# A decode attention kernel with streamed caches: the products with V eight slots later, Wq as one transfer in K's ring, Wo in fewer and larger pieces

## The chip, the core and the metric

The kernel runs on one core of a Trainium2 chip. The metric is the device time of one execution in microseconds. Three runs of the kernel before gave 201.97, 202.30 and 202.43 us (median 202.3). Times inside the text are microseconds from the start of the span of one profiled execution.

## The reference

A batch of eight tokens `x` (8 x 1 x 512) goes through a layer norm, then through two units, and the result is `x + s * g`:

```
xn = layernorm(x)
q  = xn @ wq                               # 32 heads of 128, four to each of 8 K/V heads
s  = softmax(q k^T * 128**-0.5) v @ wo     # over the last 2048 of 8192 cached positions
g  = silu((sigmoid(xn @ w_gate) * (xn @ w_up)) @ w_down)     # width 1792
out = x + s * g
```

All inputs are bf16. The windows of the two caches are 32 MB each (8 batches x 8 heads x 2048 positions x 128), Wq and Wo 4 MB each, and the three matrices of the gate 1.75 MB each: some 81 MB to be read, and little arithmetic on each byte.

## The kernel before, in words

**Tiles and rings.** K comes in eight tiles of 4 MB, K0 to K7, four to each half of the batch (four batches); a partition of a K tile is one run of 32 KB in memory. V comes in sixteen tiles of 2 MB, V0 to V15, two to each batch, with runs of 16 KB. K tiles live in a ring of three buffers of 32 KB a partition (`kring`), V tiles in a ring of four buffers of 16 KB (`vring`). Wq is read in two transfers into two of V's buffers; the gate's weights, Wd (`w_down`) and Wo follow K through K's ring. A buffer is free when the tile that was in it has been `released`, that is, when the last instruction that reads it has been put out.

**The order of loads.** All loads but x's are issued by SyncE (SP) in one queue, in an order that a sorted list fixes (lines 188 to 198): K tile i is due at slot 8i, V tiles four slots apart from the slot `PV_AT` at which their products begin. SP issues in that order and waits at each load for its buffer, so a load that waits holds back all loads behind it, in either ring. The gate's weights stand ahead of the last two V tiles, Wd and Wo at the end. Wo is read in eight pieces of 8, 8, 4, 4, 4, 2, 1 and 1 of its 32 rows a partition (1 KB a row).

**The slots.** The schedule is written by hand: one loop over slots (line 656) puts out a slot's work for every engine, in this order:

- the maximum of a K tile whose scores are complete (`soft_max_part`), and at `EXP_AT` (36 and 68) the exponentials of a batch half (`soft_exp`, ScalarE);
- just ahead of `PV_AT`, the masks (`soft_mask`, line 544, VectorE, eight instructions in two slots), which write the probabilities in the layout that the products need; there is one buffer for them, so the second half's masks wait until the first half's products are done;
- `k_turn`: one of eight in-place transposes of a K tile on VectorE (line 446); at `EXP_AT + 1`, `soft_turn`, the transposes of the probabilities;
- `qk`, four slots behind: four score products of K's tile on TensorE (line 461);
- `pv_sum` of the V tile that was completed in the slot before (TensorE line 621, then VectorE line 630), and `pv`: a quarter of the products of one V tile (line 600); after the fourth quarter ScalarE evicts the sums (line 611);
- at `EXP_AT + 2`, `soft_spread` (line 522, with evictions on ScalarE, line 530); in the slot ahead of `PV_AT`, `soft_den`, the denominators.

A V tile takes four slots, a K tile eight. In before `PV_AT` is 41 and 75: the products of the first batch half, V0 to V7, run in slots 41 to 72 beside the second half's K tiles, those of V8 to V15 from slot 75 on. Each engine works in this order, and SP's loads are put out at the end of each slot.

**Beginning and end.** The q projection (line 387) multiplies each half of Wq when it has landed; `q_out` lays the result out for the scores. After the last V tile `o_rows` lays out the attention output, `unit_out` multiplies by Wd (line 362), and 64 products with Wo (line 707) follow Wo's pieces as they land; two VectorE instructions and the store end the program.

Of the kernel before, what the change touches and what calls it, by code (L numbers as in the profile page):

```python
# [10 lines left out]
def kernel(  # L11
# [13 lines left out]
    nc = tc.nc  # L25
    P = 128
    B, _, D = A_x.shape
    _, Hkv, Sk, Dh = A_k_cache.shape
    Hq = A_wq.shape[1] // Dh
# [3 lines left out]
    KT = D // P  # L33
# [8 lines left out]
    GL = 4  # L42
    NG = Hkv // GL
# [17 lines left out]
    VSET = NT // HB  # L61
    QK_LAG = 4
    EXP_AT = [SET * (hb + 1) + QK_LAG for hb in range(HB)]
    PV_AT = [EXP_AT[0] + 5]
    for hb in range(1, HB):
        PV_AT.append(max(EXP_AT[hb] + 5, PV_AT[hb - 1] + VSET * NJ + 2))

# [36 lines left out]
    def load(dst, src, q=None):  # L104
        if q is None:
            q = nc.sync
        q.dma_start(out=dst, in_=src)  # L107

    def k_tile(shape, name):
        return kring.tile(shape, bf16, name=name, tag="kring", align_bytes=ALIGN)  # L110

    def v_tile(shape, name):
        return vring.tile(shape, bf16, name=name, tag="vring", align_bytes=ALIGN)
# [1 line left out]
    x_bf = work.tile([B, D], bf16, name="x_bf")  # L115
    nc.scalar.dma_start(out=x_bf[:], in_=A_x.flatten_outer_dims())

    wq_view = A_wq.rearrange("(p kt) n -> p kt n", kt=KT)
    KH = KT // 2
    wq_sb = []  # L120
    for kh in range(2):
        t = v_tile([P, KH, Hq * Dh], f"wq_sb{kh}")
        load(t[:], wq_view[:, kh * KH : (kh + 1) * KH, :])
        wq_sb.append(t)

    k_tiles = {}
    v_tiles = {}
# [41 lines left out]
    def load_wo():  # L169
        t = k_tile([P, KW, D], "wo_sb")  # L170
        for t0, t1 in (
            (0, 8),
            (8, 16),
            (16, 20),
            (20, 24),
            (24, 28),
            (28, 30),
            (30, 31),
            (31, 32),
        ):  # L180
            load(t[:, t0:t1, :], wo_view[:, t0:t1, :])
            for k in range(t0, t1):
                wo_parts[k] = t[:, k, :]
# [4 lines left out]
    loads = [  # L188
        (kind, i)
        for _, kind, i in sorted(  # L190
            [(KTS * i, 0, i) for i in range(NKT)]
            + [(NJ * (i % VSET) + PV_AT[i // VSET], 1, i) for i in range(NT)]
        )
    ]
    loads[-2:-2] = [(2, 0)]
    loads = loads + [(2, 1), (2, 2)]
    k_order = [x for x in loads if x[0] != 1]
    v_order = [(4, 0), (4, 1)] + [x for x in loads if x[0] == 1]
    loads_done = [0]
    released = set()  # L200

    def issue_loads():
        while loads_done[0] < len(loads):
            x = loads[loads_done[0]]
            kind, i = x
            order, n = (v_order, VRING) if kind == 1 else (k_order, KRING)
            at = order.index(x)
            if at >= n and order[at - n] not in released:
                break
            if kind == 0:  # L210
                load_k(i)
            elif kind == 1:
                load_v(i)
            else:
                (load_gate_up, load_down, load_wo)[i]()
            loads_done[0] += 1
# [40 lines left out]
    for c in range(NCOL):  # L257
        nc.tensor.matmul(
            x2_ps[32 * c : 32 * (c + 1), :],
            lhsT=ident[:B, :32],  # L260
            rhs=x_bf[:, DC * c : DC * (c + 1)],
            start=True,
            stop=True,
            tile_position=(0, 32 * c),
            skip_group_check=True,
# [3 lines left out]
    xnT_sb = work.tile([P, KT, 32], bf16, name="xnT_sb")  # L269
# [107 lines left out]
    def q_projection():  # L377
        HW = rep * Dh
        q_ps = [
            psum.tile([P, HW], f32, name=f"q_ps{gg}", tag="s_ps") for gg in range(NG)  # L380
        ]
        for kh in range(2):
            for gg in range(NG):
                for kt in range(KH * kh, KH * (kh + 1)):
                    for gl in range(GL):
                        h0 = HW * (GL * gg + gl)
                        nc.tensor.matmul(  # L387
                            q_ps[gg][32 * gl : 32 * (gl + 1), :],
                            lhsT=xnT_sb[:, kt, :],
                            rhs=wq_sb[kh][:, kt % KH, h0 : h0 + HW],  # L390
                            start=(kt == 0),
                            stop=(kt == KT - 1),
                            tile_position=(0, 32 * gl),
                            skip_group_check=True,
                        )
        return q_ps

    def q_out(gg, q_ps, on_dve):
        HW = rep * Dh
        q_sb = ppool.tile([P, HW], bf16, name="q_sb", tag="pp")  # L400
        nc.scalar.copy(  # L401
            out=q_sb[:].rearrange("p (y e w) -> p y e w", e=2, w=32),
            in_=q_ps[:].rearrange("p (y w e) -> p y e w", e=2, w=32),
        )
        qT_sb = ppool.tile([P, HW], bf16, name="qT_sb", tag="pp")
        nc.vector.transpose(out=qT_sb[:], in_=q_sb[:])  # L406
        for gl in range(GL):
            for Q in range(NQ):
                h = GL * gg + gl
                c0 = rep * NQ * (h % 2) + rep * Q  # L410
                out = qz_sb[32 * Q : 32 * (Q + 1), :, h, :, c0 : c0 + rep]
                in_ = qT_sb[32 * gl : 32 * (gl + 1), :].rearrange(
                    "p (r y b) -> p b y r", r=rep, b=32
                )[:, Q:B:NQ]
                if Q in on_dve:
                    nc.vector.tensor_copy(out=out, in_=in_)
                else:
                    nc.scalar.copy(out=out, in_=in_)  # L418

    q_tiles = q_projection()  # L420
    q_out(0, q_tiles[0], (0, 1))
    released |= {(4, 0), (4, 1)}
    issue_loads()

    s_tiles = {}
# [87 lines left out]
    def soft_spread(hb):  # L513

        pt = pt_of.pop(hb)[:].rearrange("p c (y m) -> p c y m", y=2)
        pc = ppool.tile([P, NG, NQ, CH, rep], bf16, name="pc_bf", tag="pp")
        for gg in range(NG):
            for ch in range(2):
                c = slice(CB * ch, CB * (ch + 1))
                pT_ps = psum_a.tile([P, CB, NQ, rep], f32, name="pT_ps", tag="acc_ps")  # L520
                for y in range(2):
                    nc.tensor.matmul(  # L522
                        pT_ps[:],
                        lhsT=spread[:, gg, y].rearrange("p k g -> p (k g)"),
                        rhs=pt[:, c, y, :],
                        start=(y == 0),
                        stop=(y == 1),
                        skip_group_check=True,
                    )
                nc.scalar.copy(  # L530
                    out=pc[:, gg, :, c, :].rearrange("p q c r -> p c q r"),
                    in_=pT_ps[:],
                )
        pc_of[hb] = pc

    def soft_mask(hb, gg):

        if gg == 0:
            pT_of[hb] = work.tile(
                [P, NG, NQ * CB, GL, 2 * rep], bf16, name="pT_sb", tag="pT_sb"  # L540
            )
        pc = pc_of[hb][:, gg].rearrange("p q (c e) r -> p (q c) (e r)", e=2)
        for gl in range(GL):
            nc.vector.tensor_scalar(  # L544
                out=pT_of[hb][:, gg, :, gl, :],
                in0=pc,
                scalar1=Hm[:, gl : gl + 1],
                scalar2=None,
                op0=ALU.mult,
            )  # L550
# [104 lines left out]
    KSLOT = NKT * KTS  # L655
    for t in range(PV_AT[-1] + VSET * NJ):
        u = -1
        for hb, at in enumerate(PV_AT):
            if 0 <= t - at < VSET * NJ:
# [3 lines left out]
        for hb in range(HB):  # L663
            if t == EXP_AT[hb]:
                soft_exp(hb)
            for gg in range(NG):
                if t == PV_AT[hb] - NG + gg:
                    soft_mask(hb, gg)
# [13 lines left out]
        for hb in range(HB):  # L682
            if t == EXP_AT[hb] + 2:
                soft_spread(hb)
            if t == PV_AT[hb] - 1:
                soft_den(hb)
# [18 lines left out]
    for k in range(KW):  # L705
        for c in range(NCOL):
            nc.tensor.matmul(  # L707
                a_ps[32 * c : 32 * (c + 1), :],
                lhsT=o2_sb[:, k, :],
                rhs=wo_parts[k][:, DC * c : DC * (c + 1)],  # L710
                start=(k == 0),
                stop=(k == KW - 1),
                tile_position=(0, 32 * c),
                skip_group_check=True,
# [41 lines left out]
```

## Time and profile before

| | |
|---|---|
| median of three runs | 202.3 us |
| the profiled execution's own time | 201.77 us |
| its span, first to last instruction | 200.0 us |
| mean granted TensorE clock | 0.867 |
| read from memory | 81.01 MB, 405 GB/s over the span |
| products with V begin | 84.1 us |
| first exponentials of the second half | 130.9 us |
| V8's products done (first tile of the second half) | 150.6 us |
| Wd landed, last Wo product | 186.7 us, 196.9 us |

The page shows each engine's busy time, then forty slices of 5 us with the busy tenths of each engine, the granted TensorE clock, the DMA engines' share and rate. A chain follows the last instruction back to what released it. A row of the timeline gives start, length, engine, line, operation and names; the brackets behind it say how long the engine had been idle and what ended that. An issue's time to landing is the time from the instruction on SP to the completion that consumers wait for.

### The profile page before, as it was taken

The page shows a single profiled execution, that of the slowest core. Times are in us where ns is not written, and L with a number is a line of the kernel's source. Part 1 is how long each engine was busy: PE and PEld are TensorE (multiplying, and loading weights), DVE is VectorE, ACT ScalarE, POOL GpSimd, SP SyncE. Part 2 cuts the span into 40 slices and gives each one's busy share as a digit, 9 for nine tenths or more (in the row PEclk, how much of TensorE's full clock was granted, in tenths as well). Part 3 has the DMA queues.
Part 4 walks back from the last instruction along what each step waited for, and adds up shares of the span by engine and source line. Part 5 has one row for each costly group of instructions (what it writes and reads, how often), then busy time and mean ns, then how long its engine had stood idle before and what let it go on. Part 6 is the DMA issues. An engine that isn't in the chain of part 4 may idle for free.

```text
span 200.0 us, 2312 instructions
## 1 busy us (share of the span) xinstructions
PE 99.5 (50%) x950; PEld 42.6 (21%) x950; DVE 111.3 (56%) x182; ACT 29.3 (15%) x69; POOL 1.6 (1%) x8
## 2 busy tenths in 40 slices
PE   0430024433333047399884088839467535445683
PEld 0110001101011011113331013313144422223461
DVE  4705499999999968798890749143521100030201
ACT  3015050000000344010011001161401103100000
POOL 3000000000000000000000000000000000000000
PEclk9999999999999999769999559985969985558588
DMA  6999999999999999999999999999976999999990
GB/s 238 433 478 426 420 415 420 446 459 442 433 419 420 419 420 449 456 403 420 465 426 413 423 433 429 429 421 433 406 292 272 411 421 425 432 436 419 410 402 23
DMA packets 5386, 81.16 MB, mean 406 GB/s; under 512 B 616, under 2 KB 896, under 8 KB 1408
## 3 DMA queue, kind: packets, MB, share of 16 engines
q1 hardware_dynamic: 5344, 81.01, 95.4%
q8 instruction: 7, 0.11, 0.2%
q14 instruction: 3, 0.02, 0.0%
q10 hardware_dynamic: 32, 0.01, 0.0%
HBM read 81.01 MB, written 0.01 MB: 405 GB/s over the span
## 4 chain that ended last, share of the span: by engine, by line
DMA 53%; DVE 21%; PE 17%; ACT 5%; issue 2%; SPq 1%; ACTq 0%; DVEq 0%
DMA k_sb<-in_A_k_cache_dram 19%; DMA v_sb<-in_A_v_cache_dram 13%; DVE k_sb L446 13%; DMA wo_sb<-in_A_wo_dram 11%; DMA wgu_sb<-in_B_w_up_dram 9%; PE acc_ps L600 7%; PE s_ps L461 3%; DVE pT_sb L544 3%; PE o_ps L621 3%; ACT p_bf L489 3%; PE pT_ps L522 2%; DVE pt_bf L509 1%; ACT acc_sb L611 1%; SPq L107 1%; DVE mx L475 1%
## 5 line engine op out<-in xcount | busy, mean ns | idle before, releaser
L446 DVE STREAM_TRANSPOSE k_sb<-k_sb 128x1024 f32<-128x1024 f32 x64 | 74.4, 1213 | 11.3 <-DMA k_sb<-in_A_k_cache_dram 11.2
L461 PE MATMUL s_ps<-k_sb,qz_sb 128*32 128x512 bf16 x256 | 29.8, 540 | 43.3 <-DVE k_sb L446 37.6
L600 PE MATMUL acc_ps<-v_sb,pT_sb 128*32 128x256 bf16 (+1 forms) x384 | 35.4, 366 | 16.2 <-DMA v_sb<-in_A_v_cache_dram 16.1
L630 DVE TENSOR_SCALAR o_sb<-o_ps,rden 16x128 bf16<-16x128 f32 x16 | 5.4, 338 | 37.9 <-PE o_ps L621 37.9
L461 PEld LDWEIGHTS <-qz_sb 128*32 128x32 bf16 x256 | 8.6, 112 | 69.0 <-issue 54.5
L621 PE MATMUL o_ps<-acc_sb,Sel 128*16 128x128 f32 x96 | 15.9, 311 | 9.9 <-ACT acc_sb L611 9.6
L600 PEld LDWEIGHTS <-pT_sb 128*32 128x32 bf16 (+1 forms) x384 | 13.6, 111 | 28.2 <-DMA v_sb<-in_A_v_cache_dram 17.9
L611 ACT COPY acc_sb<-acc_ps 128x512 f32<-128x512 f32 (+1 forms) x16 | 7.7, 480 | 79.6 <-PE acc_ps L600 79.6
L621 PEld LDWEIGHTS o_ps<-acc_sb,Sel 128*16 128x16 f32 x96 | 9.1, 107 | 16.5 <-ACT acc_sb L611 14.0
L544 DVE TENSOR_SCALAR pT_sb<-pc_bf,Hm 128x1024 bf16<-128x1024 bf16 x16 | 6.6, 479 | 6.2 <-PE acc_ps L600 5.7
L522 PE MATMUL pT_ps<-pt_bf,spread 128*128 128x512 bf16 x16 | 6.8, 572 | 2.1 <-DVE pt_bf L509 2.0
L475 DVE TENSOR_REDUCE mx<-s_ps 128x1 f32<-128x512 f32 x8 | 5.4, 671 | 4.4 <-PE s_ps L461 4.4
L509 DVE STREAM_TRANSPOSE pt_bf<-p_bf 128x512 bf16<-128x512 bf16 x8 | 5.0, 680 | 4.8 <-ACT p_bf L489 4.8
L489 ACT ACT_TABLE_LOAD x1 | 1.3, 1283 | 39.8 <-DVE nm L483 39.8
L387 PE MATMUL q_ps<-wq_sb,xnT_sb 128*32 128x512 bf16 x32 | 3.8, 626 | 5.7 <-DMA wq_sb<-in_A_wq_dram 2.9
L418 ACT COPY qz_sb<-qT_sb 32x32 bf16<-32x32 bf16 x20 | 4.8, 241 | 8.6 <-DVE qT_sb L406 8.3
L489 ACT ACTIVATE p_bf<-s_ps,nm 128x512 bf16<-128x512 f32 x8 | 5.4, 686 | 4.0 <-DVE nm L483 4.0
L530 ACT CAST pc_bf<-pT_ps 128x512 bf16<-128x512 f32 x8 | 4.7, 586 | 8.7 <-PE pT_ps L522 6.0
L336 PE MATMUL d_ps<-wgu_sb,xnT_sb 128*32 128x448 bf16 x32 | 3.4, 573 | 5.2 <-DMA wgu_sb<-in_B_w_up_dram 2.8
L707 PE MATMUL a_ps<-wo_sb,o_sb 128*32 128x256 bf16 x64 | 5.0, 288 | 1.4 <-DMA wo_sb<-in_A_wo_dram 1.2
L573 PE MATMUL den_ps<-ones,dh 128*16 128x1 f32 x32 | 1.4, 166 | 7.1 <-DVE dh L560 6.6
L406 DVE STREAM_TRANSPOSE qT_sb<-q_sb 128x512 bf16<-128x512 bf16 x2 | 1.4, 691 | 5.7 <-ACT q_sb L401 5.7
(59 smaller groups left out, 41.7 us busy)
## 6 DMA issues: line engine op xcount, KB each, us to landing
k_sb<-in_A_k_cache_dram SPq DMA_DIRECT2D x8, 4096.0 KB, 29.0
v_sb<-in_A_v_cache_dram SPq DMA_DIRECT2D x16, 2048.0 KB, 24.6
wq_sb<-in_A_wq_dram SPq DMA_DIRECT2D x2, 2048.0 KB, 9.5
wo_sb<-in_A_wo_dram SPq DMA_DIRECT2D x2, 1024.0 KB
wgu_sb<-in_B_w_gate_dram SPq DMA_DIRECT2D x1, 1792.0 KB, 15.0
wgu_sb<-in_B_w_up_dram SPq DMA_DIRECT2D x1, 1792.0 KB, 18.8
wd_sb<-in_B_w_down_dram SPq DMA_DIRECT2D x1, 1792.0 KB, 29.4
wo_sb<-in_A_wo_dram SPq DMA_DIRECT2D x3, 512.0 KB, 24.2
```

The source lines that it names most:

```text
L446: nc.vector.transpose(out=kw, in_=kw)
L461: nc.tensor.matmul(s_tiles[i][32 * g : 32 * (g + 1), :], lhsT=qz_sb[:, hb, h, 2 * a + e, :], rhs=kT[:, :, a, h, :, e], start=(n == 0), sto ...
L475: nc.vector.reduce_max(out=mx_of[hb][:, kq : kq + 1], in_=s_tiles[i][:], axis=AX.X)
L489: nc.scalar.activation(out=p_bf[:, :, kq], in_=s_tiles.pop(NK * hb + kq)[:].rearrange("p (o c j) -> p c j o", o=2, j=NC), func=AF.Exp, bia ...
L509: nc.vector.transpose(out=pt[:, w * n : w * (n + 1)], in_=p_bf[:, w * n : w * (n + 1)])
L522: nc.tensor.matmul(pT_ps[:], lhsT=spread[:, gg, y].rearrange("p k g -> p (k g)"), rhs=pt[:, c, y, :], start=(y == 0), stop=(y == 1), skip_ ...
L544: nc.vector.tensor_scalar(out=pT_of[hb][:, gg, :, gl, :], in0=pc, scalar1=Hm[:, gl : gl + 1], scalar2=None, op0=ALU.mult,)
L600: nc.tensor.matmul(acc_tiles[i][w * c : w * (c + 1), :], lhsT=pT[:, 16 * ch : 16 * ch + w], rhs=v_tiles[i][:, ch : ch + n_ch, :].rearrange ...
L611: nc.scalar.copy(out=acc_sb[:], in_=acc_tiles.pop(i)[:])
L621: nc.tensor.matmul(o_ps[rows, :], lhsT=Sel[16 * n_ch][:, c].rearrange("p g r -> p (g r)"), rhs=acc_sb[:, Dh * c : Dh * (c + 1)], start=(c ...
L630: nc.vector.tensor_scalar(out=o_sb[rows, b, :], in0=o_ps[rows, :], scalar1=rden_of[b // NQ][rows, b % NQ : b % NQ + 1], scalar2=None, op0= ...
L707: nc.tensor.matmul(a_ps[32 * c : 32 * (c + 1), :], lhsT=o2_sb[:, k, :], rhs=wo_parts[k][:, DC * c : DC * (c + 1)], start=(k == 0), stop=(k ...
```

## The change

Three edits, in one diff. The products with V of both halves begin eight slots later: `PV_AT` becomes 49 and 83. As the order of loads is sorted by due slots, K6 now stands ahead of V0 and V1, and K7 ahead of V2 and V3. Wq is one tile in K's ring, read by one transfer with runs of 32 KB, so all four of V's buffers are free from the start while K2 takes the buffer that Wq leaves; the q projection completes one group of heads after the other. And Wo is read in six pieces of 16, 8, 4, 2, 1 and 1 rows.

```diff
@@ -61,7 +61,8 @@
     QK_LAG = 4
     EXP_AT = [SET * (hb + 1) + QK_LAG for hb in range(HB)]
-    PV_AT = [EXP_AT[0] + 5]
+    PV_LAG = 13
+    PV_AT = [EXP_AT[0] + PV_LAG]
     for hb in range(1, HB):
         PV_AT.append(max(EXP_AT[hb] + 5, PV_AT[hb - 1] + VSET * NJ + 2))
@@ -115,13 +116,8 @@
-    wq_view = A_wq.rearrange("(p kt) n -> p kt n", kt=KT)
-    KH = KT // 2
-    wq_sb = []
-    for kh in range(2):
-        t = v_tile([P, KH, Hq * Dh], f"wq_sb{kh}")
-        load(t[:], wq_view[:, kh * KH : (kh + 1) * KH, :])
-        wq_sb.append(t)
+    wq_sb = k_tile([P, KT, Hq * Dh], "wq_sb")
+    load(wq_sb[:], A_wq.rearrange("(p kt) n -> p kt n", kt=KT))
@@ -169,10 +165,8 @@
         for t0, t1 in (
-            (0, 8),
-            (8, 16),
-            (16, 20),
-            (20, 24),
+            (0, 16),
+            (16, 24),
             (24, 28),
@@ -194,8 +188,8 @@
-    k_order = [x for x in loads if x[0] != 1]
-    v_order = [(4, 0), (4, 1)] + [x for x in loads if x[0] == 1]
+    k_order = [(4, 0)] + [x for x in loads if x[0] != 1]
+    v_order = [x for x in loads if x[0] == 1]
@@ -379,20 +373,19 @@
-        for kh in range(2):
-            for gg in range(NG):
-                for kt in range(KH * kh, KH * (kh + 1)):
-                    for gl in range(GL):
+        for gg in range(NG):
+            for kt in range(KT):
+                for gl in range(GL):
...
@@ -419,7 +412,7 @@
-    released |= {(4, 0), (4, 1)}
+    released.add((4, 0))
```

More of the change, by code (lines that the diff above doesn't have):

```diff
@@ L381, in q_projection @@
         ]
-        for kh in range(2):
-            for gg in range(NG):
-                for kt in range(KH * kh, KH * (kh + 1)):
-                    for gl in range(GL):
[L386 to L395, printed above, removed]
+        for gg in range(NG):
+            for kt in range(KT):
+                for gl in range(GL):
+                    h0 = HW * (GL * gg + gl)
+                    nc.tensor.matmul(
+                        q_ps[gg][32 * gl : 32 * (gl + 1), :],
+                        lhsT=xnT_sb[:, kt, :],
+                        rhs=wq_sb[:, kt, h0 : h0 + HW],
+                        start=(kt == 0),
+                        stop=(kt == KT - 1),
+                        tile_position=(0, 32 * gl),
+                        skip_group_check=True,
+                    )
         return q_ps
```

## The prediction

> **What bounds the kernel now.** I read the page first: busy shares, then the slices.
>
> ```profile
> PE 99.5 (50%) x950; PEld 42.6 (21%) x950; DVE 111.3 (56%) x182; ACT 29.3 (15%) x69; POOL 1.6 (1%) x8
> ...
> DMA  6999999999999999999999999999976999999990
> GB/s 238 433 478 426 420 415 420 446 459 442 433 419 420 419 420 449 456 403 420 465 426 413 423 433 429 429 421 433 406 292 272 411 421 425 432 436 419 410 402 23
> ...
> q1 hardware_dynamic: 5344, 81.01, 95.4%
> ```
>
> No compute engine is above 56%; the load queue q1 is busy 95.4%. 81 MB stream without a pause from 1.7 us to 196.3, but for one dip in slices 29 and 30. So the time is the stream plus that dip, and an edit counts only if it touches the dip, the bytes' speed, or what follows the last byte. Next the stages around the dip (columns: span, busy time of each engine, PE clock, DMA share, GB/s):
>
> ```profile
> 126.20:130.90 4.70, 4.15 (x38) 1.60 (x36) 1.34 (x4) 0.59 (x1) 0.00 (x0) 1.00 1.02 434
> 143.00:149.00 6.00, 2.51 (x38) 1.82 (x39) 3.12 (x11) 0.00 (x0) 0.00 (x0) 0.82 0.90 355
> 149.00:152.00 3.00, 2.47 (x55) 1.70 (x47) 0.57 (x2) 0.37 (x1) 0.00 (x0) 0.79 0.19 71
> 152.00:158.00 6.00, 4.19 (x91) 2.83 (x82) 0.95 (x4) 1.12 (x3) 0.00 (x0) 1.00 1.01 403
> ```
>
> The queue is idle for 6 x 0.10 + 3 x 0.81 = 3.0 us. Packets between 143 and 160 us are also longer than their kind elsewhere, by 0.95 us per DMA engine in the packet records: 3.95 us. The landings say 4.2: V10 lands at 130.8 + 14.5 = 145.3, the gate weights at 153.25 + 15.0 = 168.2, and between them V11, V12, V13 and the gate need 3 x 4.84 + 4.25 = 18.8 of those 22.9 us. I take 4.0.
>
> Why it idles, from SP's waits (first line) and the chain (start, us, what):
>
> ```profile
> SPq L107 <- PE acc_ps L600: 21.4, 4, 10.7
> ```
>
> ```profile
> 125.67 0.57 PE acc_ps L600 x4
> 129.82 0.70 DVE mx L475
> 131.51 2.20 ACT p_bf L489 x7
> 137.98 1.83 PE pT_ps L522 x4
> 141.06 1.00 PE acc_ps L600 x8
> 142.16 3.26 DVE pT_sb L544 x8
> 149.04 1.58 PE acc_ps L600 x16
> 152.66 0.53 SPq L107
> ```
>
> V12 can only be issued when V8 has left V's ring of four. V8 is the first tile of the second batch half, so it needs that half's maximum, exponentials, spread and masks, and the masks wait for V7's last product (142.07). V8 is done at 150.62 ("R" below), V12 is issued at 150.64, and bytes flow again about 1.4 us later.
>
> **The change part by part.**
>
> *Products with V eight slots later.* On SP K6 now goes ahead of V0 and V1, K7 ahead of V2 and V3; the bytes up to V4 are the same, so V4 still lands at 115.9, V3 at 111.1 and V2 at 106.2 (4.84 apart). Before, slots 61 to 68, which end K7's scores, carried V5's last and V6's products; now they carry V3 and V4. Two tiles thus move from ahead of the exponentials to between them and the masks.
>
> 1. K7's issue waits for K4's last score product, 87.3 before. DVE's eight mask instructions (2 x 1.65 us) and the denominator (1.8) now stand behind K4's and K5's transposes, so it is released near 80; K6, V0 and V1 fill the stream until 91.7. Nothing on the path.
> 2. Products begin at about 93.5 instead of 84.1: DVE runs from 75.0 through 11 transposes at 1.16, one maximum 0.65, masks 3.3 and denominator 1.9. V0 is released near 98; V4, V5, V6 and V7 wait for V0 to V3 and must be issued before 108, 113, 118 and 123. Estimated 98, 103, 109.5 and 115: at least 8 us to spare.
> 3. V3's release ("A", the place that V5's 126.24 had): V2 from 106.2 takes about 3.2 us, V3 starts at 111.2 and waits once for K7's last transpose at 113.8: A = 114.8. Bounds: 114.3 (landing plus 3.2) and 117.2 (two tiles at the 5.5 us of releases 89.4, 94.8, 100.3, 105.8); I stay near the lower, because V2's wait lets DVE run ahead.
> 4. From A through exponentials and spread to the release of the tile caught in it: 142.07 - 126.24 = 15.8 before (V7), now V5: 130.6.
> 5. Added behind it, V6 and V7: each an eviction 0.65, eight summing products 1.05, four product groups at 0.55: 3.9 us at full clock (rows at 126.32 to 128.89). At half clock 0.65 + 1.89 + 4 x 0.93 = 6.3 (rows at 134.24 and 136.13). PE is then busy for over 8 us from V5's sums on, and in before the clock came back at 140.04 after such a stretch, so I take 3.9: V7 ends at 138.4 (upper bound 143.2).
> 6. Masks to V8's release: 150.62 - 142.07 = 8.55, same instructions. R = 146.9 instead of 150.6; bounds 146.5 and 154.1.
>
> Each us that R comes earlier gives one us until the loss of 4.0 is used up, at R = 146.6. Remaining loss 0.3; gain 3.7. The later V issues have their own tiles free by 148 to 155 and are covered by more than 4 us.
>
> *Wq as one transfer.* Half the packets, twice the size. From 14 to 24 us, 128 packets of 32 KB took 97.1% of 16 x 10 us: 1.214 each; from 116 to 130, 368 of 16 KB took 0.612. So 256 x 0.612 - 128 x 1.214 = 1.3, over 16 engines 0.08 us saved. The first half's 16 products (8.09, 1.90 us) now start at 12.9: the last q product ends at 16.8 instead of 14.8, the first group's at 14.8 instead of 13.9. The wait for K0 (22.59) hides it; without that cover it costs 0.9. On SP, K2's issue now waits for the last q product, with K3 and all V behind it; K0 and K1 feed the queue until 33.2 and K3 waits until 35.2 anyway. Nothing.
>
> *Wo.* The packet records give 0.309 us for 8 KB, 0.159 for 4 KB, 0.612 for 16 KB: (256 x 0.309 - 128 x 0.612 + 256 x 0.159 - 128 x 0.309) / 16 = 0.12 us saved. Three transfers fewer save 48 completion packets of 9 ns, 0.03. The last Wo products can't start by quarters of the first half: in before 40 products ran from 190.52 to 193.51 beside landing parts, now 32 start when the first half lands, 4.84 us after Wd (186.7), which is 191.5 on before's scale, and take 2.4 us, until 193.9; rows 16 to 24 land at 194.1 as before. Last bound: 0 at full clock (76 ns a product), 1.8 at half clock (113 ns, the row of b_ps: 64 x 113 = 7.2 from 191.5 gives 198.7 against 196.9). The clock came back at 191.24 in before, after 3.7 us of products, and the new pause before them is only 0.7 us: I take 0.2.
>
> The Trainium skill ("DMA: Bandwidth & Descriptors", section Anatomy of one DMA) gives each transfer a fixed cost of about 2.0 us; by it three transfers fewer would save 6 us. The trace speaks against it here: V tiles land 4.84 us apart, 2 MB at 433 GB/s, with no room for a fixed cost while the queue is full.
>
> Sum against the profiled execution (span 200.0, 201.77 in all): 201.77 - 4.0 + 0.3 - 0.2 + 0.2 = 198.1. That execution is 0.5 below the median of the runs, 202.3; on the median's scale 198.6.
>
> **The rivals.**
>
> *One tile's worth at half clock* (20%). The same mechanism, but V6 or V7 runs at 6.3 us, or A comes at 117: R = 149.3, loss 2.7, time 201.0. For it: the clock was at half from 133 to 140 in just this stage. Against: more unbroken PE work lies there now.
>
> *The handover comes later than before: slower* (12%). Place: PE between V5's release and the masks. Both tiles at half clock (+4.8) and A at the upper bound: R = 154.1, 3.5 later than before. It decides at R = 150.8, that is if steps 3 and 5 together add over 3.9 us; then V12 is later than now. Typical R 152: 202.3 + 1.4 - 0.2 = 203.5. Against: V4 lands at 115.9 and 35 us remain for work that sums to 31.
>
> *No gain* (3%): R within 0.4 of 150.6, 202.1; the dip has only changed its tiles.
>
> *The tail loses what Wo's grain covers* (5%): half clock to the end, 198.6 + 1.6 = 200.2.
>
> *Transfers carry a fixed price after all* (1%): a V tile's packets fill 8 x 0.612 = 4.90 us of an engine; the widest spacing of V landings, 130.4 to 135.6, leaves 0.3 for each transfer, 0.9 for three: 197.7. By the skill page's 2.0 us it would be 192.6.
>
> **How the numbers follow.** Likeliest (59%): 198.6, its own range 197.4 to 199.6. The bounds are the whole 4.2 gained with no tail cost on the profiled execution's scale, and 1.3 of the loss staying. With the first rival and the tail the cases reach 201.4; outside are the slower case, no gain, and some below. Range 197.3 to 201.5. Faster by over 0.2% (my bound for what this measurement tells from no change): 0.59 + 0.20 + 0.05 + 0.01 = 0.85; same 0.03; slower 0.12.
>
> **What would show it.** The slices lose the dip or keep a shallow one; SP's wait for the product line between 140 and 160 us shrinks from 21 us; V8's last product near 147 with V12's issue at its heels; the first exponentials of the second half near 119.5 instead of 130.9; first products with V near 93; K7 issued near 80. Wrong if V6 and V7 take over 5 us each, if products begin after 96, or if the queue runs dry earlier, at V9 (needs V5's release by 132.5) or V11 (V7's by 142).

## The result, and the profile after

The changed kernel takes 199.23 us (median of four runs, 198.54 to 199.69); the kernel before, timed beside it, 202.13. The ratio is 0.986, 95% interval 0.982 to 0.990. The profiled execution of the changed kernel took 199.69 us (span 197.9), 2.1 less than that of before; it is the slowest of its four runs.

The page of the changed kernel:

```profile
PE 99.8 (50%) x950; PEld 44.4 (22%) x950; DVE 110.8 (56%) x182; ACT 29.1 (15%) x69; POOL 1.6 (1%) x8
...
DMA  6999999999999999899999999999998999999980
GB/s 227 437 464 464 424 419 424 424 424 427 424 424 437 464 470 424 374 424 474 421 411 440 421 424 427 427 426 401 411 437 344 419 431 428 436 428 431 418 360 18
...
q1 hardware_dynamic: 4912, 81.01, 96.4%
```

The engines work as much as before, on the same bytes. The dip of slices 29 and 30, counted from 0 (292 and 272 GB/s), has become one shallow slice (344), with a weak one three slices ahead of it (401). By stages (span, busy times, PE clock, DMA share, GB/s):

```profile
123.00:130.00 7.00, 5.55 (x20) 2.15 (x21) 2.76 (x5) 1.84 (x7) 0.00 (x0) 0.51 1.01 431
130.00:135.00 5.00, 4.26 (x32) 2.05 (x33) 0.34 (x1) 2.16 (x5) 0.00 (x0) 1.00 0.99 401
143.00:149.00 6.00, 4.70 (x62) 3.01 (x64) 0.78 (x4) 0.37 (x1) 0.00 (x0) 0.55 0.95 407
149.00:152.00 3.00, 2.46 (x53) 1.73 (x49) 0.34 (x1) 0.37 (x1) 0.00 (x0) 0.77 0.94 355
```

The queue now stops for 6 x 0.05 + 3 x 0.06 = 0.5 us around V12 instead of 3.0. SP's wait between 140 and 160 us and the chain through the handover:

```profile
SPq L108 <- PE acc_ps L593: 12.0, 4, 8.1
```

```profile
106.22 1.06 PE acc_ps L593 x4
107.84 0.99 PE acc_ps L593 x3
112.67 0.34 DVE o_sb L623
113.01 2.29 DVE k_sb L439 x2
115.74 0.57 PE acc_ps L593 x4
119.90 0.70 DVE mx L468
121.59 2.20 ACT p_bf L482 x7
124.32 1.89 PE o_ps L614 x8
131.14 1.00 PE acc_ps L593 x8
133.85 1.87 PE acc_ps L593 x16
137.48 1.87 PE acc_ps L593 x16
139.44 3.26 DVE pT_sb L537 x8
146.34 1.75 PE acc_ps L593 x16
```

The second half's exponentials start at 121.0 instead of 130.9; V5 is caught in the spread (its products stand among the spread's on TensorE) and leaves at 132.14, V6 and V7 follow at 3.6 us each, the masks begin at 139.44, and V8 leaves at R = 148.09 instead of 150.62. The landings say what that was worth: from V8's (135.40) to the gate weights' (166.20) the stream took 30.8 us for five V tiles and the gate, which need 5 x 4.84 + 4.25 = 28.45. So 2.35 us are still lost there: 0.9 on V9 to V11, 1.35 on V12 and 0.1 behind it. In before it was 4.2 (135.6 to 168.2).

### The profile page after: what moved, and what is told of

It is laid out like the page before. It is cut to its first block, busy times and chain, and to the rows that moved or that the text cites. A ratio compares the mean times of both kernels' runs of the same rounds, so it can differ in the third digit from the quotient of the medians.

```text
span 197.9 us, 2314 instructions
## 1 busy us (share of the span) xinstructions
PE 99.8 (50%) x950; PEld 44.4 (22%) x950; DVE 110.8 (56%) x182; ACT 29.1 (15%) x69; POOL 1.6 (1%) x8
## 4 chain that ended last, share of the span: by engine, by line
DMA 54%; PE 18%; DVE 18%; ACT 5%; issue 2%; SPq 1%; ACTq 0%; DVEq 0%
DMA k_sb<-in_A_k_cache_dram 20%; DMA wo_sb<-in_A_wo_dram 14%; DMA v_sb<-in_A_v_cache_dram 13%; DVE k_sb L439 12%; PE acc_ps L593 7%; DMA wgu_sb<-in_B_w_gate_dram 7%; PE o_ps L614 5%; PE s_ps L454 3%; ACT p_bf L482 3%; PE pT_ps L515 2%; DVE pT_sb L537 2%; ACT acc_sb L604 2%; DVE pt_bf L502 1%; DVE mx L468 1%; SPq L108 1%
## 5 line engine op out<-in xcount | busy, mean ns | idle before, releaser
L454 PE MATMUL s_ps<-k_sb,qz_sb 128*32 128x512 bf16 x256 | 29.3, 553 | 47.0 <-DVE k_sb L439 41.2
L614 PE MATMUL o_ps<-acc_sb,Sel 128*16 128x128 f32 x96 | 16.6, 321 | 10.5 <-ACT acc_sb L604 10.2
L593 PEld LDWEIGHTS <-pT_sb 128*32 128x32 bf16 (+1 forms) x384 | 14.7, 116 | 21.2 <-DMA v_sb<-in_A_v_cache_dram 8.8
```

Source lines behind the costliest of these rows:

```text
L454: nc.tensor.matmul(s_tiles[i][32 * g : 32 * (g + 1), :], lhsT=qz_sb[:, hb, h, 2 * a + e, :], rhs=kT[:, :, a, h, :, e], start=(n == 0), sto ...
L593: nc.tensor.matmul(acc_tiles[i][w * c : w * (c + 1), :], lhsT=pT[:, 16 * ch : 16 * ch + w], rhs=v_tiles[i][:, ch : ch + n_ch, :].rearrange ...
L614: nc.tensor.matmul(o_ps[rows, :], lhsT=Sel[16 * n_ch][:, c].rearrange("p g r -> p (g r)"), rhs=acc_sb[:, Dh * c : Dh * (c + 1)], start=(c ...
```

## The experiments

Theory A: the time is the stream plus what the queue loses while V's ring waits for V8's release R. Rivals: the larger transfers of Wq and Wo (B), K7's earlier place among the loads alone (C), the later slots alone (D), a loss of the queue's own that no earlier release mends (E). "Before" in a ratio is the kernel before, timed beside the run.

**Taking the parts apart.** First the products back at the old slots, Wq and Wo as changed:

```diff
-    PV_LAG = 13
+    PV_LAG = 5
```

> The changed kernel with the products back at slots 41 and 75, and with that the old order of the loads; Wq and Wo as changed. Theory A (the gain comes from V8 being released earlier, so that the queue hardly runs dry before V12): the dip comes back, V8's last product near 150.6, time 0.1 to 0.3 us under before, so 201.5 to 202.1. Theory B (the gain comes from the larger transfers of Wq and Wo): time near the changed kernel's 199.2, although the dip is back.

Measured 202.84 us, 1.005 of before (1.003 to 1.007). Its stages:

```profile
143.00:149.00 6.00, 2.48 (x38) 1.80 (x39) 3.15 (x11) 0.00 (x0) 0.00 (x0) 0.70 0.90 358
149.00:152.00 3.00, 2.47 (x38) 1.39 (x35) 0.34 (x1) 0.37 (x1) 0.00 (x0) 0.50 0.10 44
191.00:195.00 4.00, 3.10 (x30) 2.53 (x31) 0.41 (x1) 0.26 (x1) 0.00 (x0) 0.50 0.97 389
```

The dip is back whole (R 150.9) and nothing is gained, so B falls. But the time misses A's range: it is 0.9 above before, not below. Part of that is the tail: TensorE is at half clock from 191 to 195, the 64 Wo products take 5.92 us from 191.90, and the last one ends 1.0 us behind the last landing; in before it was 0.3. The two transfers alone were timed below.

Then the slots alone moved, in the kernel before:

```diff
-    PV_AT = [EXP_AT[0] + 5]
+    PV_LAG = 13
+    PV_AT = [EXP_AT[0] + PV_LAG]
```

> The kernel before with the products eight slots later and nothing else: Wq in two halves in V's ring, Wo in eight pieces. Theory A: V8's last product near 148, time 0.1 to 0.4 us above the changed kernel, 199.2 to 199.8. Theory B: near before, 201.5 to 202.3.

Measured 199.66 us (198.60 to 200.83), 0.989 of before (0.985 to 0.993), R 147.8. The interval overlaps that of the whole change. With lag5, where Wq and Wo as changed gained nothing, this puts the gain on the eight slots and the order of loads that comes with them.

**Slots against order of loads.** Moving the slots also reorders the loads. Two kernels separate these; the first keeps the old slots with the new order, the second the new slots with the old order:

```diff
-    PV_LAG = 13
+    PV_LAG = 5
-            + [(NJ * (i % VSET) + PV_AT[i // VSET], 1, i) for i in range(NT)]
+            + [(NJ * (i % VSET) + PV_AT[i // VSET] + 8, 1, i) for i in range(NT)]
```

> The changed kernel with the products at slots 41 and 75 as before, but with the loads in the changed order (K6 ahead of V0 and V1, K7 ahead of V2 and V3). Theory A with the slots as cause: the exponentials still wait for the products of V6, which lands at 125.6, V8's last product 149.5 to 150.6, time 201 to 202.1. Theory C (K7's earlier landing alone frees the handover): V8's last product near 148 and time near 199.2.

Measured 204.94 us, 1.014 (1.010 to 1.019): slower, outside both theories' ranges. The chain around 90 us:

```profile
86.64 1.07 PE acc_ps L593 x4
87.70 0.55 PE s_ps L454 x4
88.25 0.99 PE acc_ps L593 x3
89.24 0.58 PE s_ps L454 x4
89.82 0.02 issue
89.84 0.54 SPq L108
```

V0 lands late (86.6), its products hold up K4's last scores in TensorE's order, K7 is issued at 89.84 with the queue nearly empty, and from 88 to 93 us the stream runs at 242 GB/s. V2 then lands at 107.8 (96.6 in before), V3 at 112.6, and R is 153.9. C falls: K7, ahead of V2 in the queue, lands before 107.8 and so earlier than in before (111.1), but the handover comes later, because the V tiles that the old slots need come later. My expectation had left out what K7's issue waits for.

```diff
-            + [(NJ * (i % VSET) + PV_AT[i // VSET], 1, i) for i in range(NT)]
+            + [(NJ * (i % VSET) + PV_AT[i // VSET] - 8, 1, i) for i in range(NT)]
```

> The changed kernel with the products at slots 49 and 83, but with the loads in the old order (V0 and V1 ahead of K6, V2 and V3 ahead of K7). Theory A: K7 lands at 111.1, its eight transposes end near 122, the release of V3 falls near 123 instead of 116.3, V8's last product near 155, and each us of that counts in full: time 204 to 207, slower than before. Theory D (the slots alone give the gain, the order of loads is beside the point): near 199.2.

Measured 207.42 us, 1.028 (1.025 to 1.031). As A has it, K7 lands at 111.0, its last transposes end at 123.05, V3 leaves at 124.1, R is 155.9. D falls too; the queue already stops at V9, where V5 leaves at 139.9:

```profile
135.00:142.00 7.00, 5.99 (x34) 2.19 (x32) 0.34 (x1) 2.73 (x5) 0.00 (x0) 0.84 0.32 118
```

So neither alone gains at these eight slots: the gain needs later products, and K7 ahead of the V tiles that they leave for later.

**How far to move.** The same kernel with the products four and twelve slots later than before:

```diff
-    PV_LAG = 13
+    PV_LAG = 9
```

> The changed kernel with the products four slots later than before instead of eight (slots 45 and 79): V4's and V5's products share the slots with the end of K7's scores, one tile stands ahead of the masks fewer than in the changed kernel. Theory A: V8's last product between those of before (150.6) and of the change (148.1), 148.5 to 150, time 199.7 to 201.5. If the lag only moves one tile from one side of the exponentials to the other at no cost, the time is that of before.

Measured 201.51 us, 0.998 (0.996 to 1.000), R 149.6: at the upper end of the range, and with an interval up to 1.000 no gain is shown. It loses at two places, around V10 (356 GB/s from 137 to 141) and V12 (218 from 149 to 152).

```diff
-    PV_LAG = 13
+    PV_LAG = 17
```

> The changed kernel with the products twelve slots later than before (slots 53 and 87): V2's and V3's products share the slots with the end of K7's scores, and four V tiles stand between the exponentials and the masks. Theory A: while V2 waits for its landing near 106 the release that starts the handover is near 111 to 112, four tiles at 3.6 us follow, V8's last product 146.5 to 148.5, time 198 to 199.5. If TensorE's work between the exponentials and the masks has become the bound, V8's last product is at 149 or later and the time above 200.

Measured 200.90 us, 0.994 (0.993 to 0.996), above A's range and inside that of its rival, though R is 148.6 and not 149. V4 is now the tile caught in the spread; it leaves at 129.4, and V8, which waits for its buffer, is issued 1 us before V7's landing at 130.4:

```profile
127.00:132.00 5.00, 4.32 (x31) 1.95 (x31) 0.34 (x1) 2.33 (x4) 0.00 (x0) 0.95 0.62 251
```

R alone (close to the changed kernel's 148.1) does not say the time; the tile in the spread has its own deadline. Eight slots is the best of the three distances tried.

**Taking the rest of the wait away.** The masks of the second half wait for V7 because there is one buffer for all of them. Split by head group, in the same memory:

```diff
-        if gg == 0:
-            pT_of[hb] = work.tile(
-                [P, NG, NQ * CB, GL, 2 * rep], bf16, name="pT_sb", tag="pT_sb"
-            )
+        pT_of[hb, gg] = work.tile(
+            [P, NQ * CB, GL, 2 * rep], bf16, name="pT_sb", tag=f"pT_sb{gg}"
+        )
...
```

> The changed kernel with the masks' buffer split in two, one for each group of heads, in the same memory; nothing is moved. The first four mask instructions of the second half then wait for V6's last product (135.7) instead of V7's (139.4). Theory A: V8's last product 1.6 us earlier, near 146.5, of the 2.4 us that the queue still loses some 1.0 to 1.5 come back, time 197.7 to 198.5. Theory E (what is left of the loss is the queue's own, not the handover): V8 earlier, but time within 0.4 of the changed kernel.

Measured 197.77 us (197.46 to 199.41), 0.979 (0.978 to 0.981); R 145.8. The median is in A's range, against E. The profiled execution, the slowest of the five (199.41), supports A for V12 only: from V11's landing to V12's it took 4.86 us, in the changed kernel 6.19. But from V8's landing to V11's it lost 2.1 us (135.28 to 151.88 for three tiles of 4.84), where the changed kernel lost 0.9, although V9, V10 and V11 were issued at the same times to within 0.03 us. So E is not ruled out for that stretch. Then also earlier masks and denominators:

```diff
-                if t == PV_AT[hb] - NG + gg:
+                if t == PV_AT[hb] - NG + gg - 3 * hb * (1 - gg):
-            if t == PV_AT[hb] - 1:
+            if t == PV_AT[hb] - 1 - 8 * hb:
```

> As with the split buffer, and the first group's masks of the second half stand four slots earlier, the second half's denominators eight. V8's products can then follow V7's. Theory A: V8's last product 143 to 144.5, V12 issued before V11's bytes are half through, no dip, time 197.2 to 198.2, no more than 0.8 below the split buffer alone because the loss is then used up. Theory E: time within 0.4 of the changed kernel.

Measured 197.83 us (197.58 to 198.30), 0.980 (0.978 to 0.981). R is 139.9, earlier than expected, although the first group's masks stand three slots earlier by this edit and not four; no dip is left, and as expected nothing more is gained. Both beat the kernel before and the change. Two rows of each, mask_halves first (the execution of 199.41), then mask_early (197.73):

```profile
123.00:130.00 7.00, 5.55 (x20) 2.15 (x21) 2.76 (x5) 1.85 (x7) 0.00 (x0) 0.51 1.00 426
135.00:140.00 5.00, 3.57 (x32) 1.63 (x26) 2.50 (x7) 1.17 (x2) 0.00 (x0) 1.00 1.03 383
```

```profile
123.00:130.00 7.00, 5.45 (x36) 2.47 (x37) 2.47 (x5) 2.93 (x6) 0.00 (x0) 1.00 1.01 430
135.00:140.00 5.00, 4.09 (x59) 2.36 (x57) 3.94 (x10) 0.65 (x2) 0.00 (x0) 1.00 1.03 439
```

From 135 to 140 us the DMA engines of the first are as busy as those of the second (1.03) and move 13% less: single packets, the 16 KB pieces in which a V tile is moved, take longer. In the packet records this excess is 1.2 us per DMA engine between 130 and 145 us, and nearly nothing in the second. What differs upstream is the clock between 123 and 130: at half, V5's spread ends late and V9 is issued at 132.1; at full, at 129.0. That the late issue is what lengthens the packets is argued from such pairs, not shown.

**The transfers by themselves.** Wo's pieces alone, in the kernel before:

```diff
-            (0, 8),
-            (8, 16),
-            (16, 20),
-            (20, 24),
+            (0, 16),
+            (16, 24),
```

> The kernel before with Wo in six pieces (16, 8, 4, 2, 1, 1 rows) and nothing else. By the prediction's term the packets save 0.15 us and the coarser first piece costs 0 to 1.8: time 201.9 to 203.7. Theory F (the 0.9 us that the changed transfers cost at the old slots are Wo's coarser grain, paid when TensorE is at half clock after Wd): last Wo product up to 1.0 us behind the last landing instead of 0.3, time 202.3 to 203. Theory G (they are Wq's place in K's ring): within 0.2 of before.

Measured 202.09 us, 1.0008 (0.9994 to 1.0022): nothing, and the last Wo product 0.3 us behind the last landing. The clock was back at full at 191.29, before the Wo products, so this trace does not meet F's condition; the twelve runs show no such cost (201.62 to 202.41). Wq alone:

```diff
-        t = v_tile([P, KH, Hq * Dh], f"wq_sb{kh}")
-        load(t[:], wq_view[:, kh * KH : (kh + 1) * KH, :])
+    wq_sb = k_tile([P, KT, Hq * Dh], "wq_sb")
+    load(wq_sb[:], A_wq.rearrange("(p kt) n -> p kt n", kt=KT))
...
```

> The kernel before with Wq as one transfer into K's ring and nothing else. By the prediction 0.1 us saved at most: within 0.3 of before, 201.7 to 202.2. Theory G: 202.5 to 203.

Measured 202.19 us, 1.0009 (0.9995 to 1.0023): nothing either, so G falls. Two edits that are nothing alone cost 0.9 us together in the run above; half clock at the tail explains 0.7 of its profiled execution, and why all four of its runs were long stays open.

The early masks with Wo in its eight old pieces:

```diff
-            (0, 16),
-            (16, 24),
+            (0, 8),
+            (8, 16),
+            (16, 20),
+            (20, 24),
```

> The kernel with the split mask buffer and the early masks, with Wo in the eight pieces of before. Theory F: the tail is as long as with six pieces when the clock is full, up to 0.7 us shorter when it is at half; time 197.1 to 197.9 against 197.8. If the packets' size counts for more than the grain: 198 or above.

Measured 199.15 us (six runs: 197.69 and 197.86, four from 199.09 to 200.12), 0.985 (0.981 to 0.989). By the ranges this would make the old pieces worse, but the profiled execution (200.12), the slowest of the six, lost time long before Wo, with V9 issued at 132.2:

```profile
123.00:130.00 7.00, 5.57 (x21) 2.16 (x22) 2.76 (x5) 1.84 (x6) 0.00 (x0) 0.54 1.03 440
130.00:135.00 5.00, 4.32 (x35) 1.91 (x35) 0.79 (x3) 2.09 (x4) 0.00 (x0) 0.97 0.95 392
```

So the early masks do not free the kernel of V9's deadline, and their four close runs above may owe something to the clock. The pieces of Wo are not told apart by this run. Last, the early masks (Wo in six pieces) with three buffers in V's ring, to make the queue short without stopping it:

```diff
-    VRING = 4
+    VRING = 3
```

> The kernel with the split mask buffer and the early masks, with three buffers in V's ring instead of four; each V tile is issued when the tile three before it is released, by the releases of the four-buffer run 1.7 to 3 us before the queue would run dry for V8 to V10, and 5 us or more elsewhere. Theory H (packets get longer while the queue holds less than a tile, even where it never stops): no or little stop of the queue near 130 to 145, but longer packets there, 0.5 to 1.2 us in all, time 198.5 to 200.5. If length has nothing to do with the queue's depth: packets as in the four-buffer run and, with the queue's stops taken off, time within 0.5 of 197.8.

Measured 202.62 us, 1.003 (1.001 to 1.006), above both ranges. Its profiled execution (205.2 us) is longer than the median and is used for one place only: V5 left at 132.4, not 129.0, so V8's load came late and the queue stopped outright, at 165 GB/s from 128 to 134. The run does not tell short queues from stopped ones; theory H rests on the comparison of the two mask kernels and stays open.

## Why the prediction was right

Forecast 198.6 (197.3 to 201.5), measured 199.23; faster, as the likeliest case had it. The mechanism is the one forecast: V8 leaves earlier and the queue hardly stops at V12. The remaining loss came out 2 us larger than forecast, 1.2 of it because R was late, and the range was wide enough for that. Its steps:

- *What bounds the kernel*: right. In the run with the early masks, where no dip is left, the time is 197.8, so the dip was worth some 4.2 us against the 4.0 taken.
- *Step 1*: K7 issued at 79.43, near 80. *Step 2*: first product at 92.90, V0 to V3 released at 97.4, 102.8, 110.9 and 116.3 (98, 103, 109.5 and 115).
- *Step 3*: A, V3's release, is 116.3, not 114.8, inside its bounds. V2 took 4.65 us from 106.22 and not 3.2, because TensorE was at half clock when it landed: its first two quarters took 1.06 and 0.99 where I had 0.55. I had argued that V2's wait lets VectorE run ahead. It does not do so to the end: K7's last two transposes stand behind V2's sums (`o_sb` at 112.67) and end at 115.30, not 113.8. With the clock at full in the early-masks run V2 took 3.3 us and V3's release was at 115.2.
- *Step 4*: 132.14 - 116.31 = 15.83, the 15.8 taken over from before. That is partly luck: the clock was at half for 6.83 us of this stretch in both runs, and at full throughout in the early-masks run, where the stretch took 13.7:

```profile
114.67 0.57 PE acc_ps L592 x4
123.25 1.05 PE o_ps L613 x8
124.30 0.98 PE acc_ps L592 x8
127.95 1.00 PE acc_ps L592 x8
```

- *Step 5*: V6 and V7 3.6 us each, at full clock (3.9). *Step 6*: 8.74 (8.55). R is 148.1, not 146.9: V3's release 1.5 late, the two tiles 0.6 early, the masks' stretch 0.2 late.
- *The remaining loss* was mis-sized: 0.3 forecast, 2.35 measured in the profiled execution. By the prediction's own rule R = 148.1 leaves 1.5 (1.35 seen at V12). The rest, 0.9, lies at V9 to V11, where the prediction had no loss: for V9 I had named 132.5 as the latest issue. It came at 132.16, the queue hardly stopped (0.1 us), yet packets between 130 and 140 us were longer by 0.56 per engine. The packet records suggest why 132.5 is too late. The last packets of a tile end unevenly: in before, ahead of V12, 16 packets are in flight at 148.4 us, 5 at 149.1 and 2 from 150.1 to 151.6. Bytes flow some 1.4 us after an issue, and in the changed kernel only 12 to 14 are in flight at 133.6 to 133.9, 1.5 us behind V9's issue. That the long packets beside the dip would all go with it was wrong too: 0.95 us per engine in before became about 0.6 around V12 and 0.6 around V9.
- *Wq* (0.08) and *Wo* (0.15 saved, 0.2 lost at the tail): each alone shows no difference (1.0009 and 1.0008). In the changed kernel the last product ends 0.34 us behind the last landing, as in before; in the old slots with both edits it was 1.0, so the tail rival exists, at a size of 0.7.
- *The rivals*: one tile's worth at half clock (20%) came in part: V6 and V7 ran at full clock, but V2's half clock took V3's release two thirds of the way to that rival's 117. The later handover (slower, 12%) did not come in this kernel; it was seen when the loads kept their old order (R 155.9, 207.4 us). There the rule's sum, 202.0 + 5.3 = 207.3, agrees, but much of that loss stood at V9 (118 GB/s from 135 to 142 us), so the agreement does not show the rule past R = 150.8.
- *The fixed price of a transfer*: two transfers fewer in Wo and one in Wq gained nothing (1.0008 and 1.0009). The Trainium skill ("DMA: Bandwidth & Descriptors", section Anatomy of one DMA) gives the fixed 2.0 us for a DMA on GpSimd's path. The loads here are SyncE's, so the prediction took that section's figure further than it goes. An estimate with 2.0 us for each transfer would be 4 and 2 us; beside a full queue this case shows none of it.

## What to carry to other kernels

Where one queue streams without a pause, find the slot in which a ring's oldest buffer waits for work that can't start yet, and shift other work to either side of that wait. An earlier release then gives time, until the next load in the queue has its own deadline: here V8 left 2.5 us earlier, and the profiled execution was 2.1 us shorter. A schedule edit that also sorts loads is two edits: here either one alone was slower than before, and only both together gained. After such a shift, ask what the release still waits for: splitting a buffer that two groups shared, at no memory, was worth another 1.5 us by the medians (199.23 to 197.77), with one run of five at 199.41.

## What the runs showed that I had not expected

- A load issued 3 us ahead of the landing in front of it already cost time. With V9 issued at 132.1 to 132.2, 3.0 to 3.3 us ahead of V8's landing, packets of the same size took longer in the 8 us behind it and more (from 135 to 140 us 383 GB/s with the split buffer, against 439 with the early masks and V9 issued 6.6 us ahead, at the same busy share of 1.03). The cost differed, 0.9 us in the changed kernel and 2.1 with the split buffer, at the same issue times. What happens inside the engines was not seen, and why it differs is open.
- The same instructions, from V3's release to V5's, took 15.8 us in the changed kernel and 13.7 with the early masks. Eight summing products among them took 1.89 us at 124.32 in the one and 1.05 at 123.25 in the other, with the clock at 0.51 and at 1.00 from 123 to 130. The Trainium skill ("TensorE: Matmul & The Clock Gate", Part 1: The HAM clock gate) says that the window in which the clock is decided runs freely, so that the change of clock falls differently from run to run; these rows agree with it. A load that waits on TensorE inherits that spread, which may be why the four runs of the changed kernel differ by up to 1.15 us. Only the profiled executions show where it falls.
